# Four neighbouring rows of the down weights to a partition, and a step of four columns in the weight loads of gate and up

## The chip, the cores and the metric

The kernel runs on one core of one Trainium2 chip. The metric is the device time of one execution, in microseconds (us). Before the change the median of three runs is 1279.16 us (1278.78 to 1279.30).

## The reference

The program is one decode step of a transformer layer: attention over a cache of 8192 positions, then a gated feed-forward block, each behind a layer norm and with a residual. Four sequences of one token each (B = 4), a model width of 512, 32 heads of 128, and a hidden width of F = 1792 in the feed-forward block. All inputs are bf16.

```
x  = A_x                                   # [4, 1, 512]
q  = layernorm(x) @ wq                     # 32 heads of 128
p  = softmax(q . k_cache * 128 ** -0.5)    # over 8192 positions, for each sequence and head
h  = x + (p . v_cache) @ wo
g  = layernorm(h) @ w_gate                 # [4, 1792], w_gate is [512, 1792]
u  = layernorm(h) @ w_up                   # [4, 1792]
h2 = h + (sigmoid(g) * u) @ w_down         # w_down is [1792, 512]
```

## The kernel before

The two caches are 512 MB together and are read once. The kernel is written by hand for five engine queues, with an explicit semaphore for every dependency; the order of each queue is the order in which the Python code emits it. All large transfers are issued from SP, one behind the other, into a buffer KV of three slots of 64 KB to a partition. The 128 pairs of sequence and head are worked off in NG = 32 groups of four. For each group a slot receives the keys (line 286) and a slot the values (lines 293 and 295). VectorE transposes the keys in place (line 323), TensorE forms the scores (line 333) and the products with the values (line 376, and line 390 for the last group).

The change lies in the tail, behind the last group. There the order is as follows.

- `load_weights` issues the transfers of the remaining weights from SP into the slots that come free: `wo` in two halves (line 306), gate and up whole (line 310, semaphores wg and wu), and the down weights in four pieces (line 317, semaphores wd0 to wd3). The pieces are cut by `WD = ((0, 8), (8, 12), (12, 13), (13, 14))`: pieces of eight, four, one and one of NFT = 14 blocks of 128 hidden columns. In each partition a block of the down weights takes 512 numbers (1 KB).
- TensorE gathers the attention output (line 428), multiplies it with `wo` (line 438), and a layer norm follows on VectorE and ScalarE (lines 204 to 221), which leaves the normed activations, transposed, in `hnT`.
- `glu_mm` (matmuls on line 531) forms gate and then up. Both are made transposed: the weights are the stationary operand and `hnT` the moving one. For each of four chunks c of the model width and each of 14 blocks t, one instruction loads 128 columns of the weights (LDWEIGHTS, 128 x 128) and one multiplies them with four columns of `hnT` (MATMUL, 128 x 4). That is 56 pairs for gate and 56 for up.
- ScalarE takes the sigmoid of gate (line 538) while TensorE does up, and VectorE multiplies the two into `hhT` (line 540): 14 blocks of four columns, with the hidden columns of a block on the partitions.
- `f_down` multiplies `hhT` with the down weights (line 548), piece by piece, four matmuls to a block, one in each group of 32 columns of the array. Each piece waits for its own transfer.
- VectorE and ScalarE copy the result out of PSUM (lines 554 and 555), and one transfer from ScalarE's queue writes the output (line 557).

Which hidden column stands on which partition in block t is free, as long as `glu_mm` and the down weights agree. Before the change the down weights are cut so that partition x holds the 14 rows 14x to 14x + 13, one in each block. So block t of gate and up is the columns t, t + 14, t + 28 and so on: the weight loads of `glu_mm` read every fourteenth number, a step of 28 bytes.

Two other places of the same kernel load 128 columns of bf16 weights in the same way. The projection of q (`f_q`, line 247) reads them side by side, and the transposition of x (`f_xT`, line 227) reads every fourth number, in four partitions.

Of the kernel before, what the change touches and what calls it, by code (L numbers as in the profile page):

```python
# [88 lines left out]
def bass_sequential_preLN__mha_block_cached__glu_gated_glu__decode_kernel(  # L89
# [12 lines left out]
    B, _sq, D = A_x.shape  # L102
    _, H, S, DH = A_k_cache.shape
    F = B_w_gate.shape[1]
    assert DH == 128 and H == 32 and D == 512 and F == 14 * 128 and B == 4 and S == 8192
    NDC = D // 128
    NFT = F // 128
# [11 lines left out]
    with ExitStack() as es:  # L119
        def SB(name, shape, dt, **kw):  # L120
            return es.enter_context(nc.sbuf_tensor(name, shape, dt, **kw))

        def raw(t):
            return t.tensor if hasattr(t, "tensor") else t
# [23 lines left out]
        hnT = SB("hnT", [128, NDC * B], BF16)  # L148
# [6 lines left out]
        def kv(slot, off, inner, p0=0, np_=128):  # L155
            return bass.AP(raw(KV), p0 * KVROW + slot * SLOT + off, [[KVROW, np_], *inner])
# [9 lines left out]
        S_b, O_b, V_b, XB, PB, FA, FB = bank[0:2], bank[2], bank[3], bank[4], bank[5], bank[6], bank[7]  # L166
# [31 lines left out]
        def cols(t, c):  # L198
            return t[:, c:c + NDC * (B - 1) + 1:NDC]
# [103 lines left out]
        def load_weights():  # L303
            w = [t_a5[NG - 1]]
            for i in range(2):
                t_w[f"wo{i}"] = prog.dma("sp", f"wo{i}", lambda e, i=i: e.dma_start(
                    kv(1, i * 16 * D, [[1, 16 * D]]),
                    A_wo[2048 * i:2048 * (i + 1), :].rearrange("(p k) f -> p (k f)", k=16)), w)
            for kind, mat, off, lo, hi in (("wg", B_w_gate, WG, 0, NDC), ("wu", B_w_up, WU, 0, NDC)):
                t_w[kind] = prog.dma("sp", kind, lambda e, mat=mat, off=off, lo=lo, hi=hi: e.dma_start(  # L310
                    kv(1, off + lo * F, [[1, (hi - lo) * F]]),
                    mat.rearrange("(p c) f -> p (c f)", p=128)[:, lo * F:hi * F]), w)
            w = [t_pv[NG - 2]]
            for i, (lo, hi) in enumerate(WD):
                v = B_w_down.rearrange("(x t) f -> x (t f)", t=NFT)[:, lo * D:hi * D]
                dst = kv(2, lo * D, [[1, (hi - lo) * D]])
                t_w[f"wd{i}"] = prog.dma("sp", f"wd{i}", lambda e, v=v, dst=dst: e.dma_start(dst, v), w)

        def transpose_k(g, i, keep):
# [129 lines left out]
        for g in range(NG):  # L449
# [30 lines left out]
            if g == 0:  # L480
                load_k(2)
        load_weights()
        t_dm = emit("act", lambda e: e.activation(dummy[:, 0:1], TS[:, 4, 0:1], ACT.Sqrt), [t_et[NG - 1]])
        extract(NG - 2, True)
# [41 lines left out]
        def glu_mm(off, u, lo, hi):  # L526
            def f(e):
                ins = None
                for c in range(lo, hi):
                    for t in range(NFT):  # L530
                        ins = e.matmul(S_b[u][:, B * t:B * (t + 1)],  # L531
                                       kv(1, off + c * F + t, [[NFT, 128]]), cols(hnT, c),
                                       start=(c == 0 and t == 0), stop=(c == NDC - 1), skip_group_check=True)
                return ins
            return f
# [21 lines left out]
        key, v = prog.dma("act", "out", lambda e: e.dma_start(out.rearrange("b s d -> (b s) d"), o_sb), [t_o0, t_o1])  # L557
# [55 lines left out]
```

## Time and profile before

| | before |
|---|---|
| median of three runs | 1279.16 us |
| the profiled execution, its own time | 1280.09 us |
| its span, first to last instruction | 1278.3 us |
| mean granted TensorE clock | 0.907 |
| TensorE matmul busy | 998.3 us (78%) |
| TensorE weight load busy | 412.0 us (32%) |
| VectorE busy | 700.9 us (55%) |
| ScalarE busy | 84.9 us (7%) |
| HBM read | 550.77 MB, 431 GB/s over the span |
| gate and up, line 531, 112 pairs | 1267.04 to 1273.93 us |
| down, line 548, 56 pairs | 1274.29 to 1275.98 us |

The profile is of one execution. Its own time is 0.93 us above the median of the runs, and 1.79 us of it lie outside the span. PE in a profile row is a matmul on TensorE, PEld a weight load, DVE is VectorE, ACT ScalarE, and SPq the queue of SP, from which transfers are issued. The recorded ends of matmuls are modelled, their starts are not. The granted clock is a share of full speed.

### The profile page before, as it was taken

To read this page: it belongs to the slowest core of one execution; us is meant where nothing else is said; L and a number is where in the kernel's file an instruction comes from. 1 tells how busy PE (TensorE), PEld (TensorE's weight loads), DVE (VectorE), ACT (ScalarE), POOL (GpSimd) and SP (SyncE) were. 2 spreads that over 40 slices of the span, in tenths; PEclk is the share of its full clock that TensorE was granted. 3 is DMA by queue.
4 is the path that set the end of the run, shared out by engine and by line. 5 is a ranking of instruction groups with operands and counts; after the bars stand their busy time and mean duration, and the time that the engine had idled before them with its cause. 6 is when DMAs were issued, how large, how long until landed. Compare 5 with 4: busy or idle time off the path is not lost. (4 is left out here: it accounts for less than half of the span.)

```text
span 1278.3 us, 11014 instructions
## 1 busy us (share of the span) xinstructions
PE 998.3 (78%) x4486; PEld 412.0 (32%) x4486; DVE 700.9 (55%) x735; ACT 84.9 (7%) x203; POOL 22.6 (2%) x88
## 2 busy tenths in 40 slices
PE   1599777779777788777788777788777797777796
PEld 1233323333223333223333233333233333333334
DVE  0765665446655446654446654456654456654461
ACT  0000000000000000000000000000000000000010
POOL 1000000000000000000000000000000000000000
PEclk9899888899888899888998888998888998888986
DMA  9999999999999999999999999999999999999997
GB/s 421 431 424 433 441 433 427 437 437 439 427 435 433 445 427 431 435 441 433 427 439 435 439 427 437 435 441 427 435 431 441 433 427 439 437 435 429 437 433 333
DMA packets 10541, 550.95 MB, mean 431 GB/s; under 512 B 1176, under 2 KB 1440, under 8 KB 1568
## 3 DMA queue, kind: packets, MB, share of 16 engines
q1 hardware_dynamic: 10512, 550.77, 99.5%
q8 instruction: 8, 0.13, 0.0%
q14 instruction: 5, 0.04, 0.0%
q10 hardware_dynamic: 16, 0.01, 0.0%
HBM read 550.77 MB, written 0.00 MB: 431 GB/s over the span
## 5 line engine op out<-in xcount | busy, mean ns | idle before, releaser
L323 DVE STREAM_TRANSPOSE KV<-KV 128x2048 uint32<-128x2048 uint32 x256 | 568.5, 2278 | 379.3 <-DVEq L52 379.3
L333 PE MATMUL PS<-KV,Lq 128*128 128x512 bf16 x2048 | 545.5, 418 | 256.5 <-PEq L52 256.0
L376 PE MATMUL PS<-KV,PT 128*128 128x512 bf16 x1984 | 433.2, 379 | 0.0
L333 PEld LDWEIGHTS PS<-KV,Lq 128*128 128x128 bf16 x2048 | 200.4, 104 | 601.0 <-issue 443.0
L376 PEld LDWEIGHTS PS<-KV,PT 128*128 128x128 bf16 x1984 | 193.9, 98 | 234.5
L349 ACT ACTIVATE E_sb<-PS,TS 128x512 bf16<-128x512 f32 x32 | 22.0, 687 | 1124.7 <-DVE TS L348 1124.7
L343 DVE TENSOR_REDUCE TS<-PS 128x1 f32<-128x512 f32 x32 | 22.1, 691 | 70.5 <-DVEq L52 70.5
L360 ACT ACTIVATE PT<-ET 32x256 bf16<-32x256 bf16 x128 | 52.9, 414 | 30.9 <-DVE ET L352 28.5
L352 DVE STREAM_TRANSPOSE ET<-E_sb 128x512 bf16<-128x512 bf16 x32 | 22.8, 711 | 30.7 <-DVEq L52 30.7
L403 DVE STREAM_TRANSPOSE OX<-PS 128x512 f32<-128x512 f32 x31 | 20.9, 675 | 8.6 <-DVEq L52 8.6
L276 POOL TENSOR_TENSOR Lq<-q_all,mask 128x16 bf16<-128x16 bf16 x32 | 8.4, 263 | 575.3 <-DVE TS L348 563.7
L280 POOL COPY OT<-OTs 128x4 bf16<-128x4 bf16 x30 | 5.8, 192 | 622.2 <-DVE OTs L406 622.2
L247 PE MATMUL PS<-xnT,KV 128*128 128x4 bf16 x128 | 3.6, 166 | 9.3 <-DMA KV<-in_A_wq_dram 9.3
L365 DVE STREAM_TRANSPOSE TS<-TS 128x32 f32<-128x32 f32 x32 | 6.8, 211 | 6.2 <-DVEq L52 3.0
L348 DVE STREAM_TRANSPOSE TS<-TS 128x32 f32<-128x32 f32 x32 | 6.8, 212 | 4.7
L344 DVE STREAM_TRANSPOSE TS<-TS 128x32 f32<-128x32 f32 x32 | 6.8, 212 | 4.7
L406 DVE TENSOR_SCALAR OTs<-Or,small 128x4 bf16<-128x4 f32 x30 | 6.9, 229 | 4.5 <-DVEq L52 1.1
L346 DVE TENSOR_SCALAR TS<-small 128x32 f32<-128x32 f32 x32 | 5.8, 181 | 4.8 <-DVEq L52 0.2
L364 DVE COPY TS<-small 128x32 f32<-128x32 f32 x32 | 5.8, 181 | 4.7
L345 DVE TENSOR_REDUCE small<-TS 128x1 f32<-128x16 f32 x32 | 5.4, 170 | 5.1 <-DVEq L52 0.6
L405 DVE TENSOR_REDUCE Or<-OX 128x4 f32<-128x16 f32 x31 | 5.6, 179 | 4.5
L390 PE MATMUL PS<-KV,PT 128*32 128x512 bf16 x64 | 5.3, 507 | 3.5 <-issue 3.5
(81 smaller groups left out, 80.6 us busy)
## 6 DMA issues: line engine op xcount, KB each, us to landing
KV<-in_A_wq_dram SPq DMA_DIRECT2D x1, 4096.0 KB, 12.3
KV<-in_A_wo_dram SPq DMA_DIRECT2D x2, 2048.0 KB, 22.1
KV<-in_B_w_gate_dram SPq DMA_DIRECT2D x1, 1792.0 KB, 28.1
KV<-in_B_w_up_dram SPq DMA_DIRECT2D x1, 1792.0 KB, 31.9
KV<-in_B_w_down_dram SPq DMA_DIRECT2D x1, 1024.0 KB, 24.0
KV<-in_A_k_cache_dram SPq DMA_DIRECT2D x32, 32.5
KV<-in_A_v_cache_dram SPq DMA_DIRECT2D x32, 34.3
KV<-in_B_w_down_dram SPq DMA_DIRECT2D x1, 512.0 KB, 25.0
```

Of the source, the lines that this page charges most:

```text
L276: emit("pool", lambda e: e.tensor_tensor(dst, src, msk, ALU.mult), [t_q, t_mk, t_lq0, t_a5.get(g - 1), t_oc.get(g - 3)], key="lq")
L323: emit("dve", lambda e: e.transpose(v, v), key="tp", take=take, keep=keep)
L333: ins = e.matmul(S_b[0], Lq[:, hp, 15 - s:15 - s + 128], rhs, start=(s == 0 and hp == 0), stop=(s == NS - 1 and hp == 3))
L343: dv(lambda e: e.tensor_reduce(TS[:, 0, 0:1], S_b[0], AX.X, ALU.max), [t_ts0] if g == 0 else [], [("sc", 1)])
L344: dv(lambda e: e.transpose(TS[:, 1, :], TS[:, 0, :]))
L348: t_a5[g] = dv(lambda e: e.transpose(TS[:, 3, :], TS[:, 2, :]), key="dve")
L349: emit("act", lambda e: e.activation(E_sb[:, :], S_b[0], ACT.Exp, bias=TS[:, 3, 0:1], scale=SCALE, accum_out=TS[:, 4, 0:1]), [t_a5[g]], ke ...
L352: t_et[g] = dv(lambda e: e.transpose(ET[:, :], E_sb[:, :]), take=[("ex", 1)], key="dve")
L360: emit("act", lambda e, dst=dst, src=src: e.activation(dst, src, ACT.Copy), [t_et[g], t_pt0 if g < NG - 1 else t_ptl], key="pt")
L376: ins = e.matmul(O_b, PT[:, u3, off:off + 128], rhs, start=(j == 0 and rl == 0), stop=(j == 3 and rl == NS - 1))
L403: emit("dve", lambda e: e.transpose(OX[:, :, :].rearrange("p (r i) x -> p r i x", r=4), src), w, key="dv", take=take, keep=keep)
L406: t_ox[g] = emit("dve", lambda e: e.tensor_scalar(dst, Or[:, :], small[:, 2 + g % 3:3 + g % 3], None, op0=ALU.mult), take=[("dv", 1)], kee ...
```

## The change

The down weights are laid out by four neighbouring rows to a partition in place of fourteen. In the pieces of eight and of four blocks, each group of four blocks now holds 512 neighbouring rows of `w_down`, and partition x has the four rows 4x to 4x + 3 of them. The two pieces of one block hold 128 neighbouring rows, one to a partition. So a partition's part of the first piece is read from HBM as two runs of 4 KB where it was one of 8 KB; its part of the second piece stays one run of 4 KB, and of the last two one of 1 KB.

The weight loads of gate and up follow: for the blocks 0 to 11 they read every fourth number (a step of 8 bytes), for the blocks 12 and 13 numbers side by side. The number of instructions, the transfers' sizes, their order and all waits stay as they are.

```
             for i, (lo, hi) in enumerate(WD):
-                v = B_w_down.rearrange("(x t) f -> x (t f)", t=NFT)[:, lo * D:hi * D]
-                dst = kv(2, lo * D, [[1, (hi - lo) * D]])
+                if hi - lo > 1:
+                    v = B_w_down[128 * lo:128 * hi, :].rearrange("(j x k) f -> x j (k f)", j=(hi - lo) // 4, k=4)
+                    dst = kv(2, lo * D, [[4 * D, (hi - lo) // 4], [1, 4 * D]])
+                else:
+                    v, dst = B_w_down[128 * lo:128 * hi, :], kv(2, lo * D, [[1, D]])
                 t_w[f"wd{i}"] = prog.dma("sp", f"wd{i}", lambda e, v=v, dst=dst: e.dma_start(dst, v), w)
...
                 for c in range(lo, hi):
                     for t in range(NFT):
-                        ins = e.matmul(S_b[u][:, B * t:B * (t + 1)],
-                                       kv(1, off + c * F + t, [[NFT, 128]]), cols(hnT, c),
+                        j, k = divmod(t, 4)
+                        lhs = kv(1, off + c * F + 512 * j + k, [[4, 128]]) if t < 12 else kv(1, off + c * F + 128 * t, [[1, 128]])
+                        ins = e.matmul(S_b[u][:, B * t:B * (t + 1)], lhs, cols(hnT, c),
                                        start=(c == 0 and t == 0), stop=(c == NDC - 1), skip_group_check=True)
```

## The prediction

> **What bounds the kernel now.** I read the page first, for the chain that ended last and the transfers.
>
> ```profile
> span 1278.3 us, 11014 instructions
> ...
> q1 hardware_dynamic: 10512, 550.77, 99.5%
> ...
> PE 3%; DVE 0%; issue 0%; DVEq 0%; ACT 0%
> ```
>
> Up to the last group the kernel is bound by its transfers: SP's queue is busy for 99.5% of the span, and the change touches none of that. The chain that the page follows back is only the tail, a few per cent of the span. So I read that chain in order of time.
>
> ```profile
> 1267.04 6.89 PE PS L531 x112
> ...
> 1274.03 0.22 DVE E_sb L540
> ...
> 1274.29 1.69 PE PS L548 x56
> ...
> 1276.01 0.28 DVE KV L554
> ```
>
> The reader is to see that in the last ten microseconds TensorE is in the chain almost throughout, and that the 112 matmuls of gate and up (line 531) are its longest piece, 6.89 us. Down (line 548) starts 0.36 us behind them and ends at 1274.29 + 1.69 = 1275.98. What follows, the copies and the output's transfer, stays as it is.
>
> Next, what one pair of load and matmul costs at three steps between columns: 28 bytes (line 531), none (line 247, side by side) and 8 bytes (line 227). The first fence has the views by line, with shortest, median and longest duration in ns; the second the timeline. Line 227 has only four matmuls; it stands there twice, first with the two that a short window at 2.29 us catches, then with all four.
>
> ```profile
> L531 PE MATMUL PS<-hnT,KV x112: 199/199/222, 1267.0 to 1273.7; 128*128 128x4 bf16 x112
> L247 PE MATMUL PS<-xnT,KV x128: 166/166/188, 13.1 to 16.5; 128*128 128x4 bf16 x128
> L227 PE MATMUL PS<-ident,KV x4: 169/169/189, 2.2 to 2.4; 4*128 4x4 bf16 x4
> ```
>
> ```profile
> 1267.04 6.88 PE L531 MATMUL PS<-hnT,KV 128*128 128x4 bf16 x112 [0.77 <-DVE hnT L221]
> 13.12 3.58 PE L247 MATMUL PS<-xnT,KV 128*128 128x4 bf16 x128 [9.30 <-DMA KV<-in_A_wq_dram]
> 2.24 0.22 PE L227 MATMUL PS<-ident,KV 4*128 4x4 bf16 x2 [2.24 <-DMA KV<-in_A_x_dram]
> 2.24 0.29 PE L227 MATMUL PS<-ident,KV 4*128 4x4 bf16 x4 [2.24 <-DMA KV<-in_A_x_dram]
> ```
>
> A stretch less its last matmul, divided by the gaps, is the time from start to start. With 28 bytes it is (6.88 - 0.20) / 111 = 60.2 ns, side by side (3.58 - 0.17) / 127 = 26.9 ns, with 8 bytes (0.29 - 0.22) / 2 = 35 ns, to a rounding of 5. The durations say the same: they grow by 33 ns, from 166 to 199, where the spacing grows by 33, so the 169 ns of line 227 stand for some 30 ns. I take 33.
>
> Is the clock the same in these places? The recorded clock reads 1.00 in the first microseconds and 0.50 in gate and up. But the two loads of fp32 ones in the layer norms, the same code twice, take the same time in both.
>
> ```profile
> 3.22 0.50 PEld L207 LDWEIGHTS PS<-lnr,onesf 128*128 128x128 f32 x2 [0.68 <-DVE lnr L205]
> 1265.13 0.50 PEld L207 LDWEIGHTS PS<-lnr,onesf 128*128 128x128 f32 x2 [0.83 <-DVE lnr L205]
> 1257.44 0.30 PEld L415 LDWEIGHTS PS<-stx,KV 128*128 128x128 f32 x2 [1.11 <-DVE stx L414]
> ```
>
> ```profile
> 1257.00:1258.00 1.00, 0.40 (x2) 0.30 (x2) 0.48 (x3) 0.00 (x0) 0.00 (x0) 1.00 0.99 426
> 1268.00:1269.00 1.00, 1.00 (x20) 1.00 (x20) 0.00 (x0) 0.00 (x0) 0.00 (x0) 0.50 0.98 416
> ```
>
> The same two loads take 0.30 us in the stretch whose clock is 1.00 and 0.50 us at the clock of gate and up. At 3.22 us they take 0.50, so TensorE was at half clock there, whatever the record says, and it then sat idle for 9.30 us before line 247. The three prices are prices at one clock.
>
> Last, the transfers, since down waits for its weights piece by piece. Each issue is followed by its own row, which gives its size and the time from issue to landing.
>
> ```profile
> 1237.27 0.43 SPq L310 DMA_DIRECT2D KV<-in_B_w_up_dram  x1
> KV<-in_B_w_up_dram SPq DMA_DIRECT2D x1, 1792.0 KB, 31.9
> 1247.56 0.33 SPq L317 DMA_DIRECT2D KV<-in_B_w_down_dram  x1
> KV<-in_B_w_down_dram SPq DMA_DIRECT2D x1, 1024.0 KB, 24.0
> 1247.93 0.43 SPq L317 DMA_DIRECT2D KV<-in_B_w_down_dram  x1
> KV<-in_B_w_down_dram SPq DMA_DIRECT2D x1, 512.0 KB, 25.0
> 1248.89 0.42 SPq L317 DMA_DIRECT2D KV<-in_B_w_down_dram  x1
> KV<-in_B_w_down_dram SPq DMA_DIRECT2D x1, 128.0 KB, 24.6
> ```
>
> So up's weights land at 1269.17, the first piece of down at 1271.56, the second at 1272.93, the last at 1273.49. That is only 0.80 us before down starts today. This is where most of the argument lies: the shorter gate and up become, the sooner down meets weights that are not there yet.
>
> **The change part by part.** *The loads of gate and up.* Of 112 pairs 96 go from 60.2 to 33 ns and 16 (blocks 12 and 13) to 26.9 ns: 96 x 33 + 16 x 26.9 = 3.60 us in place of 112 x 60.2 = 6.74, a saving of 3.14 us on TensorE, all in the chain. The 8-byte price is the uncertain one, as it rests on four matmuls that use four rows of the array. Its bounds are the two neighbours: at 26.9 the saving is 3.73 us, at 60.2 it is 16 x 33.3 = 0.53. I take 33 because the row with that very step stands there.
>
> The Trainium skill, page "SBUF — State Buffer", section "Door 1: The DMA port swizzle", says that SBUF is read in lines of 16 bytes and that full speed needs two hits to a line. A step of 28 bytes never hits a line twice and a step of 8 always does, so by this rule 8 bytes would cost what numbers side by side cost, and TensorE would save the 3.73 us; our row for 8 bytes lies a little above that, but near it. It makes a dear 8-byte step less likely.
>
> *A new wait for up's weights.* Gate's 56 pairs take 1.80 us and end at about 1268.9. Up's weights land at 1269.17, which today is hidden behind gate. The projection of q shows what such a wait adds:
>
> ```profile
> 0.74 0.38 SPq L179 DMA_DIRECT2D KV<-in_A_wq_dram  x1
> KV<-in_A_wq_dram SPq DMA_DIRECT2D x1, 4096.0 KB, 12.3
> ```
>
> Its weights land at 13.04 and its matmuls start at 13.12, so 0.08 us. Up starts at 1269.25, its matmuls end 1.80 + 0.20 later at 1271.25, and with line 540's 0.22 and the two hand-overs of 0.03 to 0.04 down could start at 1271.55, that is 2.74 us earlier than today. The sigmoid starts when gate is done and has the whole of up to hide in, as today. Only up is queued behind the new wait on TensorE, and only line 540 waits for up.
>
> *The transfers of down.* SP issues the same four, some 24 us ahead of their landing, so a longer issue costs nothing; they queue behind up's. The second piece has runs of 4 KB as before, the last two of 1 KB. The first piece goes from runs of 8 KB to runs of 4 KB. Today its 1024 KB land 2.39 us after up's weights, 2.33 ns a KB, and the 512 KB of the second, in runs of 4 KB, take 1.37 us, 2.68 ns a KB. At the latter price the first piece takes 2.74 us, 0.35 longer. The other bound is nothing: the queue is busy 99.5% of the time, so neighbouring rows have no gap to fill. Part of the second piece's price is that it comes late, when some of the 16 engines have run out; I take 0.10. The landings become 1271.66, 1273.03 and 1273.59.
>
> *Down.* One block's four matmuls run side by side:
>
> ```profile
> L548 PE MATMUL PS<-KV,E_sb x56: 267/311/314, 1274.3 to 1275.6; 128*4 128x128 bf16 x56
> ```
>
> The 14 blocks take 1.69 us today, (1.69 - 0.31) / 13 = 0.106 each. After the change the first eight start at 1271.66 + 0.08 and are done at 1272.6. The second piece is there at 1273.11, its four blocks take until 1273.54, the third piece until 1273.64, and the last starts at 1273.59 + 0.08 = 1273.67 and ends some 0.28 later (its first matmuls take 267 ns), at 1273.95. Today it is 1275.98. The sum is 2.03 us, not 3.14: 0.4 goes to the wait for up, and the rest to the waits for down's pieces. This holds for any 8-byte price up to about 45 ns ((2.03 - 0.53) / 96 = 15.6 ns below 60.2).
>
> Against the profiled execution's own 1280.09 this is 1278.1; carried to the median of the runs, 0.93 lower, 1279.16 - 2.0 = 1277.2 us. That is 0.16%. What a measurement of this kernel can tell from no change is about 0.2%, or 2.6 us, so the likeliest case lies just within it.
>
> **The rivals.** *The transfers end sooner.* In the last two microseconds the 16 engines are unevenly loaded:
>
> ```profile
> 1271.00:1271.50 0.50, 0.50 (x11) 0.50 (x11) 0.00 (x0) 0.00 (x0) 0.00 (x0) 0.50 0.90 344
> 1271.50:1272.00 0.50, 0.50 (x12) 0.50 (x11) 0.00 (x0) 0.00 (x0) 0.00 (x0) 0.50 0.66 262
> 1272.00:1272.50 0.50, 0.50 (x11) 0.50 (x11) 0.00 (x0) 0.00 (x0) 0.00 (x0) 0.50 0.52 193
> 1272.50:1273.00 0.50, 0.50 (x11) 0.50 (x11) 0.00 (x0) 0.00 (x0) 0.00 (x0) 0.50 0.58 182
> 1273.00:1273.50 0.50, 0.50 (x12) 0.50 (x11) 0.00 (x0) 0.00 (x0) 0.00 (x0) 0.50 0.04 12
> ```
>
> The share of busy engines (the column before GB/s) falls to half. The work left at 1271.0 is 0.5 x (0.90 + 0.66 + 0.52 + 0.58 + 0.04) = 1.35 us of all engines, so spread evenly it would be done by 1272.35, 0.7 us sooner. If the new layout or the ordinary spread between executions did that, down would end at about 1273.3, close to what TensorE alone allows (1271.55 + 1.69 = 1273.24): a saving of 2.7 us, 1276.5. For it speaks that the tail is uneven; against it that nothing in the change moves work between engines. I give it 0.18.
>
> *The 8-byte step stays dear.* Beyond 45 ns a pair TensorE decides again, down to a saving of 0.53 us at 60.2: 1278.6. The four matmuls of line 227 speak against it; for it, that four rows of the array need not stand for 128. Chance 0.09.
>
> *The step is not what makes gate and up slow.* If line 247 had run at the full clock that is recorded for it, a load side by side would cost 54 ns at half clock, and 8 bytes 66: 96 x 6 less 16 x 6, or 0.5 us more, 1279.6. The Trainium skill, page "TensorE: Matmul & The Clock Gate", section "LDWEIGHTS (loading the stationary operand)", speaks for a rival of this kind: the time of a load follows from its number of columns alone, and by that the change would save nothing (1279.2). The trace is against it, with 26.9 and 60.2 ns for the same 128 columns, and the layer norm's loads show one clock. Chance 0.03.
>
> *Down's weights come late.* This is the way to a slower kernel: all 16 engines now read rows that stand side by side in HBM, and if such reads hindered each other, down's 1792 KB, 4.32 us today, would take longer, and after the change nothing covers that. The kernel is slower from a last landing of 1275.62 on, that is at 1.5 times the time, and by over 0.2% from 2.1 times; at 2.5 times the last piece lands at 1279.97, and the time is 1283.5. Against it speak the weights of gate and up, which lie side by side in HBM as well and come at 416 GB/s in the stretch from 1268 quoted above. Chance 0.05, counted as slower.
>
> **How the numbers follow.** The forecast has 0.65, its own range 1276.7 to 1277.7 (the first piece's price from 0 to 0.35, and a few tenths between executions). The range of 8 in 10 reaches down past the even transfers, 1276.2, and up into the dear step, 1278.5; it leaves out that rival's end and the two behind it. Faster by over 0.2%: 0.18 and 0.01 of the forecast's edge, 0.19. Slower: 0.05. Within: 0.76.
>
> **What would show it.** Right: the matmuls of line 531 spaced by some 33 ns, with a gap in their middle that ends with the landing of up's weights; line 548 broken up by waits for transfers, its last four matmuls right behind the last landing near 1273.6; the same length of everything before 1267 and after the copies. Wrong: spacings near 60; line 548 in one stretch of 1.7 us, which would mean that the transfers came sooner; or landings after 1274.

## The result, and the profile after

| | before | changed |
|---|---|---|
| median of 22 runs each | 1279.64 us | 1278.01 us |
| lowest and highest | 1278.78 to 1280.92 | 1277.80 to 1278.49 |
| the profiled execution, its own time | 1280.09 us | 1277.93 us |
| its span | 1278.3 us | 1276.1 us |

The changed kernel is faster by 1.63 us: the ratio is 0.9987, with a 95% interval of 0.9981 to 0.9993. That is 0.13%, within the 0.2% named in the prediction. The interval ends short of 1, so the gain is small but clear of the noise. The spread is part of the result too: 2.1 us before, 0.7 after.

Because of added lines, line 531 is line 536 in the changed kernel, 548 is 552, 317 is 320, 540 is 544. First its chain that ended last, in order of time (start, length, what):

```profile
1247.43 0.01 issue
1247.45 0.38 SPq L320
1247.83 0.04 issue
1247.87 24.96 DMA KV<-in_B_w_down_dram
1272.84 0.04 issue
1272.88 0.94 PE PS L552 x24
1273.82 0.02 issue
1273.84 0.28 DVE KV L558
```

Gate and up have left the chain. In their place stands a transfer of the down weights, the second piece, which lands at 1272.84; 0.04 us later TensorE does the last 24 matmuls of down. The bound at the end has gone from TensorE to the transfers. The timeline shows what became of the matmuls:

```profile
1267.34 3.79 PE L536 MATMUL PS<-hnT,KV 128*128 128x4 bf16 x112 [0.98 <-DVE hnT L221]
...
1271.24 0.21 DVE L544 TENSOR_TENSOR E_sb<-OX,PS 128x56 bf16<-128x56 f32 x1 [3.95 <-PE PS L536]
...
1271.68 1.02 PE L552 MATMUL PS<-KV,E_sb 128*4 128x128 bf16 x32 [0.56 <-DMA KV<-in_B_w_down_dram]
...
1272.88 0.91 PE L552 MATMUL PS<-KV,E_sb 128*4 128x128 bf16 x24 [0.17 <-DMA KV<-in_B_w_down_dram]
1273.51 0.09 PEld L552 LDWEIGHTS PS<-KV,E_sb 128*4 128x4 bf16 x4 [0.21 <-DMA KV<-in_B_w_down_dram]
```

The 112 pairs take 3.79 us where they took 6.88. Down, which was one stretch, is cut in two by its second piece, and its last four weight loads, at 1273.51, have waited for a transfer as well. The idle time before a row, in brackets, is ended by a transfer in all three places. Down ends at 1273.82, by the chain, where it ended at 1275.98.

### The profile page after: what moved, and what is told of

The parts are those of the page before. It is cut to its first block, busy times and chain, and to the rows that moved or that the text cites. A ratio compares the mean times of both kernels' runs of the same rounds, so it can differ in the third digit from the quotient of the medians.

```text
span 1276.1 us, 11014 instructions
## 1 busy us (share of the span) xinstructions
PE 992.9 (78%) x4486; PEld 407.2 (32%) x4486; DVE 701.0 (55%) x735; ACT 84.9 (7%) x203; POOL 22.7 (2%) x88
## 6 DMA issues: line engine op xcount, KB each, us to landing
KV<-in_B_w_down_dram SPq DMA_DIRECT2D x1, 1024.0 KB, 24.1
```

## The experiments

All kernels but the one for the column steps, which ran once, were timed several times beside the kernel before on the same chip. The first four shared one chip, where the kernel before had a median of 1279.27 us, and the others another, where it had 1279.36. The line numbers shift with each edit; in every timeline the rows of `128x4` behind PE are gate and up, and those of `128*4 128x128` are down.

**The changed kernel again.**

> The changed kernel again, as the measure for the kernels beside it. Theory: 1.6 us less than before (1278.0), with the same picture in the tail: pairs of gate and up every 33 ns, down waiting for its pieces.

Measured: 1278.02 us (1277.83 to 1278.24), a ratio of 0.9989 (0.9980 to 0.9998). In this execution TensorE came to gate almost 1 us sooner than in the profile above, and then the wait for up's weights shows:

```profile
1266.37 1.96 PE L536 MATMUL PS<-hnT,KV 128*128 128x4 bf16 x56 [0.77 <-DVE hnT L221]
...
1269.20 1.94 PE L536 MATMUL PS<-hnT,KV 128*128 128x4 bf16 x56 [0.88 <-DMA KV<-in_B_w_up_dram]
...
1271.26 0.21 DVE L544 TENSOR_TENSOR E_sb<-OX,PS 128x56 bf16<-128x56 f32 x1 [4.94 <-PE PS L536]
...
1271.78 1.02 PE L552 MATMUL PS<-KV,E_sb 128*4 128x128 bf16 x32 [0.63 <-DMA KV<-in_B_w_down_dram]
...
1273.61 0.09 PEld L552 LDWEIGHTS PS<-KV,E_sb 128*4 128x4 bf16 x4 [0.21 <-DMA KV<-in_B_w_down_dram]
```

TensorE waits 0.88 us between gate and up, down's last loads still start at 1273.61 against 1273.51, and the span is 1276.2 us against 1276.1. The start that was 1 us earlier gained nothing.

**The two parts of the change, each alone.** The step alone puts the two old lines back into `load_weights`:

```
-                if hi - lo > 1:
-                    v = B_w_down[128 * lo:128 * hi, :].rearrange("(j x k) f -> x j (k f)", j=(hi - lo) // 4, k=4)
...
+                v = B_w_down.rearrange("(x t) f -> x (t f)", t=NFT)[:, lo * D:hi * D]
+                dst = kv(2, lo * D, [[1, (hi - lo) * D]])
```

> The new column steps in gate and up, with the down weights laid out by fourteen rows as before (so blocks and down weights no longer belong together). Theory, that the step of the weight loads makes the gain and the landing of the down weights caps it: 33 ns a pair, waits for down's pieces, the time of the changed kernel within 0.2 us (1278.0), 0.1 less if runs of 8 KB land sooner. Rival, that the new layout of the transfers makes the gain: the time of before (1279.6).

The layout alone puts the old weight loads back into `glu_mm`:

```
-                        lhs = kv(1, off + c * F + 512 * j + k, [[4, 128]]) if t < 12 else kv(1, off + c * F + 128 * t, [[1, 128]])
...
+                                       kv(1, off + c * F + t, [[NFT, 128]]), cols(hnT, c),
```

> The new layout of the down weights, with gate and up reading every fourteenth column as before (again the two do not belong together). Theory: 60 ns a pair, down in one stretch of 1.7 us, the time of before within 0.2 us (1279.6), since the landings, 0.1 us later at most, are hidden behind gate and up. Rival, that the layout makes the gain: 1278.0.

Measured: the step alone 1277.93 us, 0.9988 (0.9979 to 0.9997); the layout alone 1279.37 us, 1.0000 (0.9991 to 1.0009). The timeline of the layout alone, from the slowest of its eleven executions (1281.04 us):

```profile
1267.93 6.88 PE L534 MATMUL PS<-hnT,KV 128*128 128x4 bf16 x112 [0.98 <-DVE hnT L221]
...
1275.19 1.66 PE L551 MATMUL PS<-KV,E_sb 128*4 128x128 bf16 x56 [0.37 <-DVE E_sb L543]
```

Gate and up take 6.88 us and down is one stretch, just as before the change. So the whole gain is that of the step in the weight loads, and the rival that the layout makes it has fallen. The runs do not tell the step alone from the changed kernel (0.1 us apart, with ranges that overlap).

**Still faster loads.** All 112 loads read side by side:

```
-                        lhs = kv(1, off + c * F + 512 * j + k, [[4, 128]]) if t < 12 else kv(1, off + c * F + 128 * t, [[1, 128]])
+                        lhs = kv(1, off + c * F + 128 * t, [[1, 128]])
```

> The changed kernel with all 112 weight loads of gate and up reading columns side by side (which no longer fits the rows of the down weights in the first twelve blocks). Theory, that the last landing of the down weights sets the end: 26.7 ns a pair, gate and up 0.6 us shorter than in the changed kernel, and the time the same within 0.2 us (1278.0). Rival, that TensorE still sets the end: 0.6 us less (1277.4).

```profile
1265.28 1.65 PE L535 MATMUL PS<-hnT,KV 128*128 128x4 bf16 x56 [0.98 <-DVE hnT L221]
...
1269.22 1.66 PE L535 MATMUL PS<-hnT,KV 128*128 128x4 bf16 x56 [2.29 <-DMA KV<-in_B_w_up_dram]
...
1270.98 0.21 DVE L543 TENSOR_TENSOR E_sb<-OX,PS 128x56 bf16<-128x56 f32 x1 [5.76 <-PE PS L535]
...
1271.80 1.02 PE L551 MATMUL PS<-KV,E_sb 128*4 128x128 bf16 x32 [0.93 <-DMA KV<-in_B_w_down_dram]
...
1273.63 0.09 PEld L551 LDWEIGHTS PS<-KV,E_sb 128*4 128x4 bf16 x4 [0.22 <-DMA KV<-in_B_w_down_dram]
```

Measured: 1278.01 us, 0.9989 (0.9980 to 0.9999). Gate and up take 1.65 us each, 0.6 less together than the 1.96 and 1.94 above, and the time does not move. The last loads start at 1273.63. Gate started 2 us sooner than in the first profile of the changed kernel, but that, and the half of the 0.6 us that lies in gate, went into the wait for up's weights (2.29 us). So only the half that lies in up could test whether TensorE sets the end, and not the 0.6 us written down for the rival. That half did reach the end of up: the product of gate and up (line 543 here, 544 there) starts at 1270.98, against 1271.26 in the repetition. It was then lost in the wait for down's first piece, for down starts at 1271.80 here and at 1271.78 there. So a shorter up gains nothing, which speaks against TensorE as the bound.

**No transfers of down.** The four transfers are left out, and so is the wait for them:

```
-                t_w[f"wd{i}"] = prog.dma("sp", f"wd{i}", lambda e, v=v, dst=dst: e.dma_start(dst, v), w)
...
-            t_d = emit("pe", f_down, [t_hh, t_w[f"wd{i}"]])
+            t_d = emit("pe", f_down, [t_hh])
```

> The changed kernel without the four transfers of the down weights: down multiplies with what lies in the slot and waits for no transfer. Theory, that the last landing sets the end: down starts as soon as its other operand is there, in one stretch of 1.7 us, and since up still waits for its weights to land at 1269.15 it ends near 1273.2, 0.6 to 0.7 us sooner than in the changed kernel: 1277.3. Rival, that something behind down sets the end: 1278.0.

```profile
1267.09 4.11 PE L528 MATMUL PS<-hnT,KV 128*128 128x4 bf16 x112 [0.77 <-DVE hnT L221]
...
1271.57 1.66 PE L544 MATMUL PS<-KV,E_sb 128*4 128x128 bf16 x56 [0.37 <-DVE E_sb L536]
...
1273.28 0.59 DVE L550 CAST KV<-PS 4x128 bf16<-4x128 f32 x2 [1.77 <-PE PS L544]
```

Three pieces of its chain that ended last show what stands behind the down weights:

```profile
1237.27 31.90 DMA KV<-in_B_w_up_dram
...
1269.22 1.99 PE PS L528 x56
...
1271.57 1.69 PE PS L544 x56
```

Measured: 1277.68 us (1277.48 to 1278.07), 0.9987 (0.9978 to 0.9996). Down is one stretch again and the copies behind it start at 1273.28, where they start at 1273.84 in the changed kernel: 0.56 us sooner in the profiles, where 0.6 to 0.7 was expected. In the medians it is 0.34 against the repetition, which ran on the other chip, and 0.26 against the control further down, which ran on this one. The direction is that of the theory, the size smaller. It says that the down weights hold the changed kernel up by no more than about half a microsecond, and that the landing of up's weights, with TensorE's work on up and down behind it, is next.

**What a column step costs.** Each of the eight chunks of gate and up got a step of its own, on a line of its own:

```
+                        if 4 * u + c == 0:
+                            ins = e.matmul(dst, kv(1, off + c * F + t, [[2, 128]]), x, **kw)
+                        elif 4 * u + c == 1:
+                            ins = e.matmul(dst, kv(1, off + c * F + t, [[4, 128]]), x, **kw)
...
```

> The kernel before with eight other column steps, one for each of the eight chunks of gate and up: 2, 4, 5, 6 in gate and 7, 8, 12, 16 in up (4 to 32 bytes; the products are then not those of gate and up). Theory, that a load pays for each 16-byte line that gives it fewer than two numbers: about 27 ns a pair at 2, 27 to 33 at 4, then rising from 5 to 8, and 60 at 8, 12 and 16, where every number is in a line of its own. Rival, that every step but one costs the same because two numbers can't be read at once: 33 ns, or 60, at all eight. Second rival, that the cost follows the span of the read: still rising from 8 to 16.

The timeline, lines 534 to 548 for the steps 2, 4, 5, 6, 7, 8, 12 and 16:

```profile
1265.28 0.51 PE L534 MATMUL PS<-hnT,KV 128*128 128x4 bf16 x14 [1.16 <-DMA KV<-in_B_w_gate_dram]
1265.65 0.61 PE L536 MATMUL PS<-hnT,KV 128*128 128x4 bf16 x14
1266.12 0.70 PE L538 MATMUL PS<-hnT,KV 128*128 128x4 bf16 x14
1266.68 0.80 PE L540 MATMUL PS<-hnT,KV 128*128 128x4 bf16 x14
...
1269.27 0.91 PE L542 MATMUL PS<-hnT,KV 128*128 128x4 bf16 x14 [1.78 <-DMA KV<-in_B_w_up_dram]
1270.04 1.00 PE L544 MATMUL PS<-hnT,KV 128*128 128x4 bf16 x14
1270.90 1.00 PE L546 MATMUL PS<-hnT,KV 128*128 128x4 bf16 x14
1271.76 1.02 PE L548 MATMUL PS<-hnT,KV 128*128 128x4 bf16 x14
```

The differences of the starts, where two chunks follow each other without a gap, divided by 14, give the price of a pair. Step 2: 0.37 / 14 = 26 ns. Step 4: 0.47 / 14 = 34 ns. Step 5: 0.56 / 14 = 40 ns. From the lengths, less the last matmul (186, 193, 200, 200 and 202 ns by the view of one line) and over 13 gaps: step 6 47 ns, step 7 55 ns, steps 8, 12 and 16 62 to 63 ns. The granted clock reads 0.50 in a stretch taken from each of the eight, so these are prices at one clock. So the price is that of side by side at 2 (3 was not run), rises by some 7 ns a step from 4 to 8, and is flat again from 8 on, as it is 60 at 14. That is the shape of the first theory; both rivals have fallen, the one of a single price and the one of a price that keeps rising. The steps 12 and 16 also show that from 8 on nothing is left to lose. Step 4 lies just above the 27 to 33 ns that were expected for it. The one timed execution took 1279.05 us.

**Half of the engines.** The attempt to make the last landing sooner. Down's pieces come in another order, and one piece goes out in sixteen transfers of eight partitions. I took such a transfer to use only half of the 16 engines; no view here counts the engines that it used.

```
-        WD = ((0, 8), (8, 12), (12, 13), (13, 14))
+        WD = ((0, 8), (12, 14), (8, 11), (11, 12))
...
+                if lo == 12:
+                    for p in range(0, 128, 8):
+                        v = B_w_down[1536 + 2 * p:1536 + 2 * (p + 8), :].rearrange("(x k) f -> x (k f)", k=2)
+                        dst = kv(2, lo * D, [[1, 2 * D]], p, 8)
```

> The changed kernel with down's pieces in the order 0-7, 12-13, 8-10, 11 and with the piece 12-13 (two neighbouring rows to a partition) cut into sixteen transfers of eight partitions each, so that only half of the engines carry it. If the half that is ahead at the end carries it: the last landing comes some 0.6 us sooner, and the time falls to 1277.4. If it is the half that is behind: the last landing comes some 0.6 us later, and the time rises to 1278.6. If the end does not hang on the last landing: 1278.0.

The control has the same order with that piece in one transfer:

> The control for the kernel with half of the engines: the same order of pieces and the same two rows to a partition in blocks 12 and 13, with that piece in one transfer over all engines. Every theory: the time of the changed kernel within 0.2 us, 1278.0, since as many bytes land last.

```profile
1271.68 1.24 PE L556 MATMUL PS<-KV,E_sb 128*4 128x128 bf16 x40 [0.61 <-DMA KV<-in_B_w_down_dram]
1273.21 0.60 PE L556 MATMUL PS<-KV,E_sb 128*4 128x128 bf16 x16 [0.30 <-DMA KV<-in_B_w_down_dram]
```

That is down in the control. In the kernel with half of the engines down looks so; the second fence has two stretches of its wait, the third the issue of the two pieces behind the sixteen transfers, with the time from issue to landing of each:

```profile
1272.13 1.02 PE L559 MATMUL PS<-KV,E_sb 128*4 128x128 bf16 x32 [1.05 <-DMA KV<-in_B_w_down_dram]
1275.26 0.55 PEld L559 LDWEIGHTS PS<-KV,E_sb 128*4 128x4 bf16 x24 [2.40 <-DMA KV<-in_B_w_down_dram]
1275.27 0.81 PE L559 MATMUL PS<-KV,E_sb 128*4 128x128 bf16 x24 [2.11 <-DMA KV<-in_B_w_down_dram]
```

```profile
1273.00:1274.00 1.00, 0.15 (x8) 0.00 (x0) 0.00 (x0) 0.00 (x0) 0.00 (x0) 0.50 0.39 96
1274.00:1275.00 1.00, 0.00 (x0) 0.00 (x0) 0.00 (x0) 0.00 (x0) 0.00 (x0) 0.50 0.22 36
```

```profile
1256.97 2.68 SPq L327 DMA_DIRECT2D KV<-in_B_w_down_dram  x2
KV<-in_B_w_down_dram SPq DMA_DIRECT2D x1, 384.0 KB, 18.5
KV<-in_B_w_down_dram SPq DMA_DIRECT2D x1, 128.0 KB, 18.1
```

Measured: 1280.25 us (1280.15 to 1280.66) with half of the engines, 1277.94 for the control, so 2.3 us later. TensorE waits 2.11 us for the piece, and while it waits the 16 DMA engines are busy for 0.39 and 0.22 of the time (the column before GB/s). It is the second case that was written down, but almost four times as large as expected. Whether the engines that carry the piece are those that are behind, or short transfers on few engines are simply slow, these runs do not tell apart. There is a third possibility: the edit also makes SP late. The sixteen issues take it until 1256.9, so the two pieces behind them go out from 1256.97 on and land at about 1275.5, where the control has issued all four pieces by 1249.3. The runs do show that a later landing is paid in full now: 2.3 us of delay in the time, with TensorE idle. A version that beats the changed kernel did not come of it; the control is not to be told from the changed kernel.

## Why the prediction was right, and where it was off

*The price of a step of 8 bytes* (33 ns, taken from four matmuls of line 227 against bounds of 26.9 and 60.2) was right. The whole of gate and up is (3.79 - 0.17) / 111 = 32.6 ns a pair, where the forecast's mix of 96 at 33 and 16 at 26.9 is 32.1. TensorE saved 3.09 us of the 3.14 worked out. The time says little about this price, since any price up to 45 ns gave the same end; the spacing is what shows it. The argument for one clock at the start and at the end held as well: side by side, gate cost (1.65 - 0.17) / 55 = 26.9 ns a pair at the end, as line 247 did at the start. The dear step did not come, and the rival in which the step is not the cause is out: the layout with the old step is as slow as before.

*The cap by the landing of the down weights* was right: down ended at 1273.82 (forecast 1273.95) and, in the repetition, where gate started 1 us sooner, at 1273.92; the gain of 2.16 us to that point is not the 3.09 that TensorE saved. The kernels with side-by-side loads and with no transfers of down show it from two sides. The new wait for up's weights is there or not, by when TensorE comes to gate: 0.88 us in one profile, 2.29 in another, none in the first, where gate started at 1267.34 and not at 1267.04.

*The first piece of down* was taken to land 0.10 us later for its shorter runs. It landed no later that one could see: the issue and landing rows of the changed kernel are

```profile
KV<-in_B_w_down_dram SPq DMA_DIRECT2D x1, 1024.0 KB, 24.1
KV<-in_B_w_down_dram SPq DMA_DIRECT2D x1, 512.0 KB, 25.0
KV<-in_B_w_down_dram SPq DMA_DIRECT2D x2, 128.0 KB, 24.7
```

with 24.0, 25.0 and 24.7 before. That term was as good as zero: with the step alone, which keeps the long runs, the first piece takes 24.1 us too, and the time is the same.

*The carry to the median* is the step that was off, by 0.8 us: 1278.01 where 1277.2 was forecast, above the forecast's own range of 1276.7 to 1277.7. Against the profiled execution the sum was 1278.1, and the changed kernel's profiled execution took 1277.93, its median 1278.01. But I then took off 0.93 us because the profiled execution of before lay that far above the median of the three runs shown. That difference was the spread of the kernel before: its 22 runs go from 1278.78 to 1280.92. The median of the first three lay 0.48 us below that of all 22, and the profiled execution 0.45 above it, with eight of the 22 longer still. Subtracting it from the changed kernel supposed that this one spreads in the same way, and its end hangs on the landing. That 1278.01 still lies in the range of 8 in 10 is in part luck, for the room above 1277.7 was left for a dear step, which did not come. What differs from execution to execution is the tail of TensorE in front of gate. Here are the stretches from 1251 to 1256 and from 1260 to 1264, with the granted clock as the third number from the end, in the changed kernel, in its repetition and with side-by-side loads:

```profile
1251.00:1256.00 5.00, 5.00 (x50) 2.03 (x53) 0.00 (x0) 0.00 (x0) 0.00 (x0) 0.50 1.03 439
1260.00:1264.00 4.00, 3.34 (x36) 1.02 (x34) 0.42 (x2) 0.00 (x0) 0.00 (x0) 0.59 1.03 441
```

```profile
1251.00:1256.00 5.00, 3.98 (x78) 2.35 (x78) 0.97 (x2) 0.00 (x0) 0.00 (x0) 1.00 0.99 426
1260.00:1264.00 4.00, 2.19 (x24) 0.58 (x24) 0.89 (x2) 0.60 (x1) 0.00 (x0) 0.50 1.03 434
```

```profile
1251.00:1256.00 5.00, 4.98 (x64) 2.35 (x67) 0.00 (x0) 0.00 (x0) 0.00 (x0) 0.67 1.03 439
1260.00:1264.00 4.00, 2.42 (x46) 0.94 (x38) 1.25 (x4) 0.60 (x1) 0.00 (x0) 1.00 1.02 434
```

The mean clock of the same code is 0.50, 1.00 and 0.67 in the first stretch and 0.59, 0.50 and 1.00 in the second, and gate starts at 1267.34, 1266.37 and 1265.28 (1267.04 in the profile of before, 1267.93 with the layout alone). A full clock early on is not all kept: in the repetition TensorE then waits 1.67 us for the second half of `wo`.

```profile
1260.72 1.88 PE L441 MATMUL PS<-KV 128*4 128x512 bf16 x16 [1.67 <-DMA KV<-in_A_wo_dram]
```

Where gate and up set the end, the start of gate goes straight into the time: spans of 1278.3 and 1279.2 us for starts at 1267.04 and 1267.93. Where the landing sets it, spans of 1276.1, 1276.2 and 1276.2 us stand beside starts 2 us apart. That the runs without a profile spread for the same reason is inferred from this, not shown. If so, the gain isn't one number: it is what a slow or a quick execution of before leaves above the landing.

*The rivals.* The even transfers did not come: the landings, counted from the issues, are those of before, and down is not in one stretch. Their forecast time of 1276.5 had the fault of the carry in it too: without transfers of down, down ended at 1271.57 + 1.69 = 1273.26, where this rival put it (1273.24), and the median was 1277.68. The 0.7 us that the prediction gives them is what they would have taken off the end of down (1273.95 to 1273.24); their landing itself would have come 1.1 us sooner (1273.49 to 1272.35). The late transfers did not come either. Had they come, they would have cost in full, as the kernel with half of the engines shows.

## What to carry to other kernels

When a stretch of small matmuls is bound by its weight loads, look at the step between the columns of the stationary operand: here, at a granted clock of 0.50, a pair cost 27 ns side by side, 33 at 8 bytes and 60 to 63 from 16 bytes on, and the layout of the matrix that consumes the result could be changed to shorten the step at no cost. Before booking such a gain, look for the transfer that lands last behind it: of 3.1 us saved, 2.2 were left in the profiles and 1.6 in the medians. And where one kernel ends on a stretch whose clock varies and the other on a transfer, compare each with its own spread, and do not carry the offset of one profile over.

## What the runs showed of the hardware that I had not expected

The price of a weight load rises evenly between the side-by-side price and the flat end: from 34 to 40, 47, 55 and 62 ns for steps of 4, 5, 6, 7 and 8 numbers, about 7 ns a step. That fits a load that is paid by the 16-byte stretches of memory that it touches, up to one for each column; no run here shows that this is the reason. The Trainium skill, page "SBUF — State Buffer", section "Door 1: The DMA port swizzle", gives 16-byte lines with full speed from two hits to a line. Here the end of the rise at 8 numbers, 16 bytes, agrees with the line; the 33 ns at two hits do not quite agree with full speed, which would be the 27 ns of numbers side by side.
